# All of the first layer's d_ff blocks by seven products instead of eight, in two interleaved groups, with V and the added exps kept once

## The chip, the cores and the metric

One core of a Trainium2 chip runs the whole program. The metric is the device time of one execution, in microseconds; the kernel before was timed three times.

## What is computed

Attention with RMS-normed q and k, then a two-layer network with a tanh GELU on the attention's output. Eight batches of 12 heads, 448 positions and 64 channels; d_model is 768, d_ff is 2048.

```python
q_n, k_n = (rmsnorm(q, g_q), rmsnorm(k, g_k))
scores = scale * np.matmul(q_n, k_n.transpose(0, 1, 3, 2))
attn = np.exp(scores - np.max(scores, axis=-1, keepdims=True))
attn = attn / (np.sum(attn, axis=-1, keepdims=True) + 1e-09)
x = np.matmul(attn, v)        # heads side by side: 3584 tokens of 768
h = x @ w_in
g = 0.5 * h * (1.0 + np.tanh(c * (h + 0.044715 * h * h * h)))
out = g @ w_out
```

## The kernel before

**Stages.** The program goes batch by batch (0 to 7), in an order written out by hand for every engine (manual_schedule): a batch's attention, then its first layer (x times w_in, GELU). The second layer of the tokens that are already through the first one is spread in small pieces over the next batch's attention, to keep TensorE filled while ACT computes exps. At the very end stands a second-layer block of its own (`final`), for the last 512 tokens.

**Attention.** Heads come in three groups of four (c = 0 to 2). Each group has seven score tiles ("units" 0 to 20 over the batch): four matmuls on 64x64 quarters of the array (L335) write a PSUM tile, ACT turns it into exps (L343). DVE adds six of the seven exp tiles of a group into `es` (steps A, B, F, G: L355, L358, L360, L362), so that the sums over keys take few matmuls (L387 with `ones`); then L387 with `vb` multiplies exps and V, and DVE divides (L397 to L422) and writes x transposed to `xT`. `STEADY` is the order of these steps on TensorE; in it, "5r" stands for five steps of the second layer (L495, four matmuls each), and "u" for a unit. A steady attention begins "5r u 11r uu": five second-layer steps, then unit 0.

**PSUM.** Four tiles of two banks, `rounds`, go round. `pair()` hands out the one that was taken longest ago; a matmul that writes it waits until its last reader is through. The second layer takes the first tile off the list for as long as it accumulates.

**First layer from batch 2 on** (class `Seven`). Eight of 16 blocks of d_ff (0 to 3 and 8 to 11) go by Strassen's scheme in Winograd's form: with w_in and x cut into 2x2 parts, seven products of 12 narrow matmuls (128x224 out, L625) take the place of eight. The sums of w_in parts are formed once (`in_sums`, in `wx`, and `in_place_sum`), the four sums of x parts per batch (`x_sums`, L610 to L613, in `xs`). Products are accumulated in PSUM tiles: X holds product 1, then 1+6, then 1+6+7, then 1+6+7+4; Y holds product 2, Z holds products 5 and 3. ACT copies X at three of these points to SBUF ("keep", L636, into `snaps`), DVE adds copies to Y and Z (L684, L695, L703), and ACT takes four GELUs (L640). The other eight blocks are four `lone` pairs, plain matmuls 448 columns wide (L652, GELU in L658). `early` issues the parts of them that need only the first two thirds of x, while the last third is still being divided; `rest` goes on with the remaining third, and calls side steps by number (`side(0)` to `side(17)`): the work for the next batches that is put between.

**Side work in a first layer of batch b.** Batch b+1's q and k are normed by GpSimd (L278, six operations) and turned by DMA (L319); DVE scales k by the gains (`gain`, L325). Batch b+2's q and k are squared (L162 on ACT, L164 on GpSimd) and totalled on DVE (L173). GpSimd runs its queue in order, and is held back by tiny copies (`gpsimd_waits`, L1035) that read a result it shall not overtake. V is loaded from GpSimd's queue (L147) into `vb`, two tiles in turn, a batch ahead.

**The end.** `token_sums` and `weight_sum` form on DVE the sums for seven products in the last second-layer block (L881 to L884, L873, L875); `final` multiplies (L914) and adds.

Of the kernel before, what the change touches and what calls it, by code (L numbers as in the profile page):

```python
# [17 lines left out]
def kernel(  # L18
# [37 lines left out]
    exq = ctx.enter_context(tc.tile_pool(name="exq", bufs=2))  # L56
    xp = ctx.enter_context(tc.tile_pool(name="xp", bufs=1))
# [51 lines left out]
    vb = [wts.tile([P, HP, NT, D], BF16, name=f"vb{i}") for i in range(2)]  # L109
# [35 lines left out]
    def load_v(b, i, n):  # L145

        nc.gpsimd.dma_start(  # L147
            vb[b % 2][:, i:i + n].rearrange("p a t d -> p a (t d)"),
            v[b, 2 * i:2 * (i + n)].rearrange("(a r) (p t) d -> (r p) a (t d)", r=2, t=NT),
        )  # L150
# [200 lines left out]
    def add_exps(b, c, step):  # L351
        ex = exs[b, c]
        if step == "A":
            es = ess[b, c] = exq.tile([P, 2, 2, S], BF16, tag="es", name="es")
            nc.vector.tensor_add(es, ex[:, :2], ex[:, 2:4])  # L355
# [15 lines left out]
    def products(b, c, what, lo=0, hi=NT):  # L371
# [11 lines left out]
        for i in range(lo, min(hi, n)):  # L383
            for r in range(2):
                rs = slice(r * R, (r + 1) * R)
                for a in range(2):
                    nc.tensor.matmul(  # L387
                        o[r][a * D:(a + 1) * D],
                        vb[b % 2][rs, 2 * c + a, i] if what else ones[rs], es[i][rs, a],
# [180 lines left out]
    wx = wts.tile([128, 3, NCH, FS * 128], BF16, name="wx")  # L570
    fs1, fs2 = slice(0, FS * 128), slice(d_ff // 2, d_ff // 2 + FS * 128)
    LONE = (2, 3, 6, 7)

    def in_sums():

        a11, a21, a12, a22 = wv[:, 0, :, fs1], wv[:, 0, :, fs2], wv[:, 1, :, fs1], wv[:, 1, :, fs2]
        nc.vector.tensor_sub(wx[:, 1], a21, a11)
        nc.vector.tensor_add(wx[:, 0], wx[:, 1], a22)
        nc.vector.tensor_sub(wx[:, 2], a12, wx[:, 0])

    def in_place_sum():

        a21 = wv[:, 0, :, fs2]
        nc.vector.tensor_add(a21, a21, wv[:, 1, :, fs2])

    class Seven:

        def __init__(self, b):
# [6 lines left out]
            self.snaps = [  # L595
                flat[:, n + i * 4 * S:n + (i + 1) * 4 * S].bitcast(F32)
                .rearrange("p (r s) -> p r s", r=2) for i in range(2)
            ]
# [5 lines left out]
            self.lhs = {1: wv[:, 0, :, fs1], 2: wv[:, 1, :, fs1], 4: wv[:, 1, :, fs2],  # L604
                        5: wv[:, 0, :, fs2], 6: wx[:, 0], 7: wx[:, 1], 3: wx[:, 2]}
# [9 lines left out]
        def product(self, i, name, ms=range(NCH)):  # L615
            first = name not in self.tiles
            if first:
                self.tiles[name] = pair("h7")
                self.owner[name] = i
            t, owner = self.tiles[name], self.owner[name]  # L620
            for bank in range(2):
                for n in range(2):
                    at = (bank * 2 + n) * 128
                    for m in ms:
                        nc.tensor.matmul(  # L625
                            t[:, bank, n * QS:(n + 1) * QS],
                            self.lhs[i][:, m, at:at + 128], self.rhs[i][:, m],
                            start=i == owner and n == m == 0,
# [6 lines left out]
        def keep(self, n):  # L635
            nc.scalar.copy(self.snaps[n], self.of("X"))  # L636

        def gelu(self, src, half, tokens):
            lo = self.b % 2 * S + tokens * QS
            nc.scalar.activation(  # L640
                g[:, half * nf // 2:half * nf // 2 + FS, lo:lo + QS],
                src.rearrange("p r (n s) -> p r n s", n=2), AF.Gelu_apprx_tanh,
            )

        def lone(self, i, js, cs, end=False):
            if i not in hs1:
                hs1[i] = pair("hh")
            h = hs1[i]
            for j in js:
                at = (2 * i + j) * 128  # L650
                for c in cs:
                    nc.tensor.matmul(  # L652
                        h[:, j, :S], win[:, c, at:at + 128], xT[self.b][:, c],
                        start=(c == 0), stop=(c == HP - 1),
                    )
            if end:
                lo = self.b % 2 * S
# [664 lines left out]
```

## Time and profile before

| what | us |
|---|---|
| median of three runs (lowest, highest) | 385.64 (385.57, 385.95) |
| the profiled execution | 384.59 |
| its span, from first to last instruction | 382.8 |
| granted TensorE clock, mean | 0.999 |
| a steady first layer (batch 4) | 17.33 |
| a steady attention with second-layer steps (batch 5) | 27.00 |
| first layers of batches 2 to 7 | 17.32 to 17.37 |

The span is split into 40 slices on the page; TensorE is busy for 90% or more in all but the first, second and last. Busy here is the matmul row, whose ends are modelled. The chain of waits is TensorE for 92% of the span, so most other engines' idle time costs nothing by itself. In the lists below a row gives start, length, engine, source line, operation, what is written and read, shapes and count; a bracket at its end gives the idle time before it and who ended that.

### The profile page before, as it was taken

The page shows a single profiled execution, that of the slowest core. Times are in us where ns is not written, and L with a number is a line of the kernel's source. Part 1 is how long each engine was busy: PE and PEld are TensorE (multiplying, and loading weights), DVE is VectorE, ACT ScalarE, POOL GpSimd, SP SyncE. Part 2 cuts the span into 40 slices and gives each one's busy share as a digit, 9 for nine tenths or more (in the row PEclk, how much of TensorE's full clock was granted, in tenths as well). Part 3 has the DMA queues.
Part 4 walks back from the last instruction along what each step waited for, and adds up shares of the span by engine and source line. Part 5 has one row for each costly group of instructions (what it writes and reads, how often), then busy time and mean ns, then how long its engine had stood idle before and what let it go on. Part 6 is the DMA issues. An engine that isn't in the chain of part 4 may idle for free.

```text
span 382.8 us, 14538 instructions
## 1 busy us (share of the span) xinstructions
PE 374.9 (98%) x6508; PEld 273.6 (71%) x6508; DVE 299.4 (78%) x441; ACT 289.6 (76%) x358; POOL 134.1 (35%) x118
## 2 busy tenths in 40 slices
PE   8899999999999999999999999999999999999995
PEld 5565577677878858886678867788678866778563
DVE  4999969995999758895789956996588833899853
ACT  6995589777997689877897789966897659965500
POOL 5997504349203850057401861038400640000000
PEclk9999999999999999999999999999999999999999
DMA  8999999978913996259832897139553340220023
GB/s 255 324 236 210 210 238 235 275 152 190 245 48 77 223 203 112 59 109 260 184 90 53 193 252 117 45 89 222 112 98 84 74 96 15 74 63 3 2 61 105
DMA packets 64594, 54.48 MB, mean 142 GB/s; under 512 B 37652, under 2 KB 60436, under 8 KB 64532
## 3 DMA queue, kind: packets, MB, share of 16 engines
q1 hardware_dynamic: 54016, 41.04, 42.8%
q0 software_dynamic: 10128, 11.80, 18.5%
q8 instruction: 51, 0.84, 0.9%
q10 hardware_dynamic: 388, 0.72, 0.5%
q14 instruction: 11, 0.09, 0.1%
HBM read 45.61 MB, written 11.01 MB: 148 GB/s over the span
## 4 chain that ended last, share of the span: by engine, by line
PE 92%; ACT 5%; DMA 1%; DVE 0%; issue 0%; POOL 0%
PE t L495 33%; PE t L652 14%; PE t L625 13%; PE t L387 9%; PE t L335 8%; PE t L537 5%; PE t L914 5%; ACT ex L343 4%; PE t L556 4%; DMA rawq<-in_q_dram 1%; PE h L436 1%; PE tp L296 1%; PE o L387 0%; DVE ss L173 0%; POOL nrmq L278 0%
## 5 line engine op out<-in xcount | busy, mean ns | idle before, releaser
L343 ACT ACTIVATE ex<-t,shift 128x896 bf16<-128x896 f32 x168 | 156.7, 1013 | 2.9 <-PE t L335 2.2
L495 PE MATMUL t<-wout,g 64*64 64x384 bf16 (+1 forms) x3456 | 150.6, 305 | 0.0
L495 PEld LDWEIGHTS <-g 64*64 64x64 bf16 x3456 | 104.4, 107 | 29.2 <-issue 2.2
L335 PE MATMUL t<-qT,kT 64*64 64x448 bf16 x672 | 57.5, 351 | 1.4 <-ACT ex L343 0.6
L652 PE MATMUL t<-xT,win 128*128 128x448 bf16 x288 | 58.5, 353 | 0.0
L173 DVE TENSOR_REDUCE ss<-sq 128x14 f32<-128x896 f32 (+3 forms) x45 | 43.5, 995 | 18.5 <-ACT sq L162 16.1
L1035 POOL COPY mark<-es 1x1 bf16<-1x1 bf16 x7 | 1.2, 177 | 128.2 <-DVE es L362 119.8
L652 PEld LDWEIGHTS <-win 128*128 128x128 bf16 x288 | 27.7, 98 | 24.1 <-issue 2.1
L278 POOL TENSOR_TENSOR nrmq<-rawq,rinv 128x896 bf16<-128x896 f32 (+1 forms) x21 | 35.4, 1688 | 19.2 <-ACT rinv L205 10.6
L355 DVE TENSOR_TENSOR es<-ex 128x1792 bf16<-128x1792 bf16 x21 | 22.3, 1061 | 16.3 <-ACT ex L343 16.3
L278 POOL TENSOR_TENSOR nrmk<-rawk,rinv 128x896 bf16<-128x896 f32 (+1 forms) x21 | 34.6, 1647 | 0.0
L397 DVE STREAM_TRANSPOSE st<-t 128x448 f32<-128x448 f32 x42 | 24.8, 629 | 10.5 <-PE t L387 9.7
L387 PE MATMUL t<-ex,vb 64*64 64x448 bf16 x588 | 32.3, 350 | 0.0
L335 PEld LDWEIGHTS <-kT 64*64 64x64 bf16 x672 | 23.7, 106 | 9.4 <-issue 1.4
L625 PEld LDWEIGHTS <-win 128*128 128x128 bf16 x288 | 27.6, 98 | 2.7 <-issue 1.0
L658 ACT ACTIVATE g<-t 128x896 bf16<-128x896 f32 x24 | 22.0, 916 | 9.3 <-PE t L652 9.3
L387 PEld LDWEIGHTS <-vb 64*64 64x64 bf16 x672 | 23.3, 107 | 7.9 <-issue 1.2
L409 DVE STREAM_TRANSPOSE rb<-rc 128x896 f32<-128x896 f32 (+1 forms) x25 | 26.7, 1067 | 0.3
L636 ACT COPY xs<-t 128x896 f32<-128x896 f32 x18 | 16.3, 906 | 13.0 <-PE t L625 10.5
L422 DVE TENSOR_TENSOR xT<-t,rb 128x896 bf16<-128x896 f32 x21 | 22.8, 1086 | 0.9
L513 ACT COPY osb<-t 128x768 f32<-128x768 f32 (+1 forms) x18 | 12.6, 703 | 14.0 <-PE t L495 14.0
L164 POOL TENSOR_TENSOR sq<-rawk 128x896 f32<-128x896 f32 (+1 forms) x14 | 22.6, 1614 | 0.7 <-DMA rawk<-in_k_dram 0.7
(147 smaller groups left out, 529.3 us busy)
## 6 DMA issues: line engine op xcount, KB each, us to landing
rawq<-in_q_dram SPq DMA_DIRECT2D x22, 448.0 KB, 4.3
rawk<-in_k_dram SPq DMA_DIRECT2D x22, 448.0 KB, 5.7
out_dram<-osb SPq DMA_DIRECT2D x38, 192.0 KB, 2.9
vb<-in_v_dram POOLq DMA_DIRECT2D x6, 672.0 KB, 7.6
win<-in_moe_w_in_dram POOLq DMA_DIRECT2D x8, 384.0 KB, 11.6
out_dram<-osb SPq DMA_DIRECT2D x31, 96.0 KB, 2.5
wout<-in_moe_w_out_dram POOLq DMA_DIRECT2D x3, 768.0 KB, 18.0
vb<-in_v_dram POOLq DMA_DIRECT2D x2, 448.0 KB, 16.4
```

Of the source, the lines that this page charges most:

```text
L164: eng.tensor_mul(sq, raw, raw)
L173: nc.vector.reduce_sum(sss[b][:, seat(b, c), "qk".index(n), hs, ts], squares(b, c, n, hs, ts), axis=AX.X)
L278: eng.tensor_mul(nrms[n, b, c][:, ts].rearrange("p t a d -> p a t d"), raws[n, b, c][:, :, ts], root[:, :, ts].to_broadcast([P, 2, m, D]),)
L335: nc.tensor.matmul(sc[r * R:(r + 1) * R, a, :S], kT[rs, c, t, r], qT[b][rs, c, :, r], start=True, stop=True,)
L343: nc.scalar.activation(exs[b, c][:, t], scs.pop((b, c, t))[:, :, :S], AF.Exp, scale=scale, bias=shift)
L387: nc.tensor.matmul(o[r][a * D:(a + 1) * D], vb[b % 2][rs, 2 * c + a, i] if what else ones[rs], es[i][rs, a], start=(i == 0), stop=(i == n ...
L397: nc.vector.transpose(st[:, r].rearrange("p a b -> p (a b)"), o[r])
L409: nc.vector.transpose(oas["rb"][:, rs].rearrange("p r s -> p (r s)"), rc.to_broadcast([128, (rs.stop - rs.start) * m, 32]),)
L422: nc.vector.tensor_mul(xT[b][:, 2 * c:2 * c + 2], oas["o", c, 1][:, :, :S], oas["rb"])
L495: mm = nc.tensor.matmul(o[a * R:(a + 1) * R, bank, :hi - lo], g[rs, f, at:at + R], wout[rs, f, lo:hi], start=(n == 0), stop=(n == len(step ...
L625: nc.tensor.matmul(t[:, bank, n * QS:(n + 1) * QS], self.lhs[i][:, m, at:at + 128], self.rhs[i][:, m], start=i == owner and n == m == 0, s ...
L652: nc.tensor.matmul(h[:, j, :S], win[:, c, at:at + 128], xT[self.b][:, c], start=(c == 0), stop=(c == HP - 1),)
```

## The change

- `wx` doubles, and the 16 blocks form two groups, A (blocks 0 to 3 and 8 to 11) and B (4 to 7 and 12 to 15). Both go by seven products; the lone pairs are gone. The products of A and B alternate; a name such as XA is tile X of group A, and "6XA" below is product 6 accumulated into it. Z takes over the tile of Y (`on=`). Each group has three keeps, three adds and four GELUs; group B's copies lie in a further exp tile (`more_snaps`, called `sn`).
- The sums of w_in for B are formed behind those for A, ahead of attentions 1 and 2.
- `vb` and `es` exist once; V is loaded in the attention that uses it, from GpSimd's queue.
- Two of three q and k tiles are squared by GpSimd: c = 0 stays on ACT, q of c = 1 moves from ACT to GpSimd.
- In the next batch's norming, k of c = 0 moves behind the small copy that waits for `xs`; the first DMA transpose and the loads behind it move from side step 2 to 5.
- Of the last block's sums of w_out, two are formed ahead of attention 7; all token sums stand behind the last add of the first layer. Their homes change, as `vb` is one tile now.

```diff
-    vb = [wts.tile([P, HP, NT, D], BF16, name=f"vb{i}") for i in range(2)]
+    vb = wts.tile([P, HP, NT, D], BF16, name="vb")
...
-            es = ess[b, c] = exq.tile([P, 2, 2, S], BF16, tag="es", name="es")
+            es = ess[b, c] = esp.tile([P, 2, 2, S], BF16, tag="es", name="es")
...
+    def in_sums(grp):
+        f1, f2 = blocks_of(0, grp), blocks_of(1, grp)
+        a11, a21, a12, a22 = wv[:, 0, :, f1], wv[:, 0, :, f2], wv[:, 1, :, f1], wv[:, 1, :, f2]
+        s2, s3, s4 = wxs[grp]
+        nc.vector.tensor_sub(s3, a21, a11)
+        nc.vector.tensor_add(s2, s3, a22)
+        nc.vector.tensor_sub(s4, a12, s2)
...
-    def product(self, i, name, ms=range(NCH)):
+    def product(self, i, name, ms=range(NCH), on=None):
         first = name not in self.tiles
         if first:
-            self.tiles[name] = pair("h7")
+            if on:
+                t = self.tiles[on]
+                rounds.append(rounds.pop(next(n for n, x in enumerate(rounds) if x is t)))
+            self.tiles[name] = self.tiles[on] if on else pair("h7")
...
     def early(self):
-        hs1.clear()
         two = range(NCH - 1)
-        self.lone(LONE[0], range(2), early)
-        self.product(1, "X", two)
-        self.product(2, "Y", two)
+        for i, name in ((1, "XA"), (2, "YA"), (1, "XB")):
+            self.product(i, name, two)
...
+            product(1, "XA", one)
+            keep("XA", 0)
+            product(1, "XB", one)
+            keep("XB", 0)
+            product(2, "YA", one)
+            add("YA", 0)
+            product(2, "YB")
+            gelu("YA", 0, 0)
+            product(6, "XA")
+            keep("XA", 1)
+            add("YB", 0)
+            product(6, "XB")
+            keep("XB", 1)
+            gelu("YB", 0, 0)
             side(5)
+            product(5, "ZA", on="YA")
+            product(7, "XA")
+            keep("XA", 0)
+            add("ZA", 0, self.snaps["A"][0])
+            product(7, "XB")
+            keep("XB", 0)
+            self.gelu_kept("A")
             side(8)
+            product(5, "ZB", on="YB")
+            add("ZB", 0, self.snaps["B"][0])
+            self.gelu_kept("B")
+            product(3, "ZA")
+            add("ZA", 1)
+            gelu("ZA", 0, 1)
             side(11)
+            product(4, "XA")
+            gelu("XA", 1, 0)
+            product(3, "ZB")
+            add("ZB", 1)
+            gelu("ZB", 0, 1)
             side(15)
+            product(4, "XB")
+            gelu("XB", 1, 0)
             side(17)
...
-            extra += [("first", lambda: gain(2, 2)), ("first", in_place_sum)]
+            extra += [("first", lambda: gain(2, 2)), ("first", lambda: in_place_sum("A")), ("first", lambda: in_place_sum("B"))]
...
-                   (0, lambda: normed_both(b + 1, 0, nc.gpsimd)),
+                   (0, lambda: normed(b + 1, 0, "q", nc.gpsimd)),
                    (0, lambda: gpsimd_waits(sevens[b].xs[:1, 3, 0, :1])),
+                   (0, lambda: normed(b + 1, 0, "k", nc.gpsimd)),
...
-                m1 += [(15, lambda a=a: squared(b + 2, 1, "q", a)) for a in range(2)]
-                m1.append((15, lambda: square(b + 2, 1, "k", nc.gpsimd)))
-                m1 += [(17, lambda n=n: total(b + 2, 1, n)) for n in "qk"]
+                for c in (1, 2):
+                    m1 += [(11, lambda c=c, n=n: square(b + 2, c, n, nc.gpsimd)) for n in "qk"]
+                m1 += [(11, lambda: total(b + 2, 1, "q")), (17, lambda: total(b + 2, 1, "k"))]
...
-            m1 += [(5, sums_homes), (5, lambda: weight_sum(3)), (5, lambda: weight_sum(2)),
-                   (11, lambda: weight_sum(4)), (17, lambda: token_sums(slice(2, 6))),
-                   (17, lambda: token_sums(slice(0, 2)))]
+            m1 += [(5, lambda: weight_sum(4)), (17, lambda: token_sums(slice(0, 2))),
+                   (17, lambda: token_sums(slice(4, 6))), (17, lambda: token_sums(slice(2, 4)))]
+        if b + 2 == B:
+            extra += [("first", sums_homes),
+                      ("first", lambda: weight_sum(3)), ("first", lambda: weight_sum(2))]
```

What the order becomes is shown at two places. The first is ACT's queue from the last GELUs of batch 2's first layer to the first exps of attention 3; t_100, t_101, t_893 and t_894 are the four PSUM tiles, and each exp reads the tile that its unit wrote. Before:

```order
L640 ACTIVATE g<-t_894 128x4x224
L658 ACTIVATE g<-t_101 128x2x448
L162 ACTIVATE sq<-rawq 128x448 x2
L658 ACTIVATE g<-t_100 128x2x448
L658 ACTIVATE g<-t_893 128x2x448
L1278 ACT_TABLE_LOAD
L343 ACTIVATE ex<-t_101,shift 128x896
L343 ACTIVATE ex<-t_100,shift 128x896
```

Now, where the four tiles are t_103 (YA, then ZA), t_104 (XA), t_895 (XB) and t_896 (YB, then ZB):

```order
L666 ACTIVATE g<-t_103 128x4x224
L666 ACTIVATE g<-t_104 128x4x224
L666 ACTIVATE g<-t_896 128x4x224
L666 ACTIVATE g<-t_895 128x4x224
L1304 ACT_TABLE_LOAD
L344 ACTIVATE ex<-t_895,shift 128x896
L344 ACTIVATE ex<-t_103,shift 128x896
```

Unit 0's tile was that of the GELU third from last; now it is that of the very last one, t_895. The second place is DVE's queue in the same first layer, from the add into the kept copy (`xs`, `sn`) to the first add of exps of the next attention. Before:

```order
L695 TENSOR_TENSOR xs<-t_894,xs 128x896
L703 TENSOR_TENSOR t_894<-t_894,xs 128x2x448
L173 TENSOR_REDUCE ss<-sq 128x14 x2
L325 TENSOR_SCALAR kT<-kT,gcols 128x896
L173 TENSOR_REDUCE ss<-sq 128x14 x2
L325 TENSOR_SCALAR kT<-kT,gcols 128x896
```

Now:

```order
L661 TENSOR_TENSOR xs<-t_103,xs 128x896
L661 TENSOR_TENSOR sn<-t_896,sn 128x896
L661 TENSOR_TENSOR t_103<-t_103,xs 128x2x448
L174 TENSOR_REDUCE ss<-sq 128x14
L661 TENSOR_TENSOR t_896<-t_896,sn 128x2x448
L174 TENSOR_REDUCE ss<-sq 128x14
L326 TENSOR_SCALAR kT<-kT,gcols 128x896
L174 TENSOR_REDUCE ss<-sq 128x14 x2
L326 TENSOR_SCALAR kT<-kT,gcols 128x896
```

A total (L174) of the tile that GpSimd squares now stands between the last two adds (L661 on t_103, that is ZA, and on t_896, ZB); before, both totals stood behind all the adds.

170 lines of the change are left out of this document (73 added, 97 removed).

## The prediction

> **What bounds the kernel now.** I read the page's first part, then busy time by stage (batch 4's first layer, then attention 5; batches count from 0), then that first layer engine by engine.
>
> ```profile
> PE 374.9 (98%) x6508; PEld 273.6 (71%) x6508; DVE 299.4 (78%) x441; ACT 289.6 (76%) x358; POOL 134.1 (35%) x118
> 209.78:227.11 17.33, 17.33 (x137) 12.66 (x140) 12.59 (x15) 12.72 (x17) 12.39 (x9) 1.00 0.88 211
> 227.11:254.11 27.00, 27.00 (x694) 20.46 (x694) 22.64 (x31) 24.20 (x29) 3.96 (x5) 1.00 0.45 98
> ```
>
> TensorE fills both stages (after the length, the columns are PE, PEld, DVE, ACT, POOL, clock), so matmul time taken out counts, unless a wait takes its place. ACT fills 24.20 of 27.00 us of attention: it has little room to start late. The timeline of TensorE in that first layer (start, length, engine, line):
>
> ```profile
> 209.72 1.69 PE L652 MATMUL t<-xT,win 128*128 128x448 bf16 x8
> 211.24 2.46 PE L625 MATMUL t<-xT,win 128*128 128x224 bf16 x24
> 213.54 0.92 PE L652 MATMUL t<-xT,win 128*128 128x448 bf16 x4
> 226.57 0.54 PE L652 MATMUL t<-xT,win 128*128 128x448 bf16 x2
> 227.04 1.01 PE L495 MATMUL t<-wout,g 64*64 64x384 bf16 x20
> 227.88 0.36 PE L335 MATMUL t<-qT,kT 64*64 64x448 bf16 x4
> ```
>
> Eight 448-column matmuls issue in 211.24-209.72 = 1.52 us, 0.190 each. The 24 narrow ones issue from 211.24 until L652 follows at 213.54: 2.30 us, 0.0958 each; their results are there at 213.70, 0.16 after that. The stage runs from 209.72 to 227.04, and unit 0, the first score matmul of the next attention, starts at 227.88, 18.16 us after the stage began. That last number is the yardstick below.
>
> **The saving on TensorE.** The stage's 84 narrow and 48 wide matmuls become 168 narrow ones: 168x0.0958 = 16.09 us against 17.32, so 1.23 us less in each of six batches, 7.4 us in all. Whether it arrives is a question of who must finish before unit 0.
>
> The Trainium skill (TensorE: Matmul & The Clock Gate, Back-to-back issue gap) says that streams of weight load and matmul settle at about 81 ns for 128 columns and 131 ns for 512. Read linearly between these, an estimate by that page, 224 columns take 94 ns and 448 take 123, so 168 narrow ones would cost 15.7 us and the old mix 13.8: a loss of 1.9 us a batch. The rows above have 190 ns for 448, so the trace disagrees and the saving on TensorE stands.
>
> **Unit 0 in batches 2 to 5.** With both groups in flight all four PSUM tiles stay in use to the end, and unit 0 writes the tile of XB, the last to be read: ACT's last gelu must end first. Before, it wrote a tile that ACT had emptied at 224.33. ACT and DVE rows of the stage:
>
> ```profile
> 211.81 1.03 ACT L162 ACTIVATE sq<-rawk 128x448 f32<-128x448 f32 x2
> 213.36 0.91 ACT L636 COPY xs<-t 128x896 f32<-128x896 f32 x1 [0.51 <-PE t L625]
> 222.61 0.92 ACT L640 ACTIVATE g<-t 128x896 bf16<-128x896 f32 x1 [0.77 <-DVE t L703]
> 223.42 0.91 ACT L658 ACTIVATE g<-t 128x896 bf16<-128x896 f32 x1
> 227.15 0.92 ACT L658 ACTIVATE g<-t 128x896 bf16<-128x896 f32 x1 [1.08 <-PE t L652]
> 229.38 1.01 ACT L343 ACTIVATE ex<-t,shift 128x896 bf16<-128x896 f32 x1
> 211.17 1.09 DVE L422 TENSOR_TENSOR xT<-t,rb 128x896 bf16<-128x896 f32 x1
> 212.29 1.05 DVE L610 TENSOR_TENSOR xs<-xT 128x672 bf16<-128x672 bf16 x1
> 213.38 0.51 DVE L611 TENSOR_TENSOR xs<-xT,xs 128x672 bf16<-128x672 bf16 x1
> 214.64 1.09 DVE L684 TENSOR_TENSOR t<-t,xs 128x896 f32<-128x896 f32 x1
> 215.64 1.07 DVE L173 TENSOR_REDUCE ss<-sq 128x14 f32<-128x896 f32 x1
> ```
>
> They give the prices: a gelu lasts 0.92 and lets the next start after 0.81; a keep (L636) 0.91; a PSUM add 1.09, and the next DVE operation may start after 1.00; ACT starts 0.04 after TensorE's end (227.11 to 227.15), which I use behind DVE too. TensorE starts 0.06 after what it waited for (60.42 to 60.48, rows further down). By hand, in the trace's clock:
>
> - TensorE: 24 early matmuls to 212.02; then the third chunk of xT, ready at 212.26, so on at 212.32 (0.30 lost). The first parts of XA, XB and YA end at 213.47, then eleven products of 1.15: YB, 6XA, 6XB, 5ZA, 7XA, 7XB, 5ZB, 3ZA, 4XA, 3ZB, 4XB; 3ZB's results are there at 225.13, 4XB's at 226.28.
> - The rereads between them just fit. ACT's squares end at 212.84, so keep XA runs to 213.8, before 6XA at 214.62; the gelu of YA ends at 216.1, before 5ZA at 216.92; the other keeps have about 1 us. The three keeps and three adds that a batch gains lie beside matmuls here.
> - DVE then has add ZA, the total of q's second tile, and add ZB in its queue. That total waits for a GpSimd square, which used to be ACT's:
>
> ```profile
> 214.99 1.68 POOL L278 TENSOR_TENSOR nrmq<-rawq,rinv 128x896 bf16<-128x896 f32 x1
> 216.64 1.68 POOL L278 TENSOR_TENSOR nrmk<-rawk,rinv 128x896 bf16<-128x896 f32 x1
> 221.73 1.67 POOL L164 TENSOR_TENSOR sq<-rawk 128x896 f32<-128x896 f32 x1
> 213.00 1.22 SPq L319 DMA_TRANSPOSE kT<-nrmk  x1
> rawq<-in_q_dram SPq DMA_DIRECT2D x22, 448.0 KB, 4.3
> vb<-in_v_dram POOLq DMA_DIRECT2D x6, 672.0 KB, 7.6
> 241.47 1.52 PE L387 MATMUL t<-ex,vb 64*64 64x448 bf16 x28
> ```
>
> Behind the wait for xs, four normings take 221.73-214.99 = 6.74, a single one 1.65 to the next. That wait ends some 0.55 earlier (L610 drops from 1.05 to about L611's 0.51, as GpSimd no longer runs a norming beside it), but five normings follow it: 214.44+6.74+1.65 = 222.83, and the square ends at 224.50. The total runs 224.53 to 225.60, so add ZB starts at 225.52 instead of 225.17 and ends at 226.61; gelu ZB starts at 226.65, gelu XB at 227.46, ending at 228.38; unit 0 starts at 228.44. If the normings keep 1.65 throughout, all this is 0.13 earlier. So unit 0 comes 0.43 to 0.56 later than its old 227.88, with all of the saved 1.23 us gone into a wait. I take +0.50 for each of four batches: **+2.0 us**. Bounds: with no total in the way +0.21 (+0.8 in all); with the load of that square late, more: it goes out behind the k transpose, which waits for the first of the five (214.44+1.68+1.22, about 217.4), lands 4.3 us later by the median, 221.7, and is used at 222.83, so it has 1.1 us to spare; I allow a lateness of 1.2 beyond that (+6.8).
>
> Behind unit 0, exp 0 follows the last gelu by 1.31 us as before (228.07 to 229.38), so at 229.69: 1.25 us behind its matmul, where it was 1.50 behind, so attention takes no longer than before. V's load now falls in the batch that uses it: issued behind the last square at about 229.5, landing 7.6 us later, at 237.1, and first used by matmuls at 241.47, before any delay: hidden, 0. The single es tile costs 0: its next writer stands behind DVE transposes that already wait for its readers.
>
> **Batch 6** has no squares or totals: add ZB starts at 225.17, unit 0 at 228.09: **+0.2**. The w_out sums moved ahead of attention 7 (four halves, by L875's 1.75 for a whole one under 1 us each) start about 1 us before unit 0 and end about 2 us before exp 3 does, which DVE waits for: 0, and up to 2 us if DVE got to them later.
>
> **Attentions 1 and 2.** The sums for group B go on DVE ahead of the first add of exps:
>
> ```profile
> 53.17 0.96 DVE L579 TENSOR_TENSOR wx<-win,wx 128x1536 bf16<-128x1536 bf16 x1
> 55.62 1.09 DVE L355 TENSOR_TENSOR es<-ex 128x1792 bf16<-128x1792 bf16 x1 [1.49 <-ACT ex L343]
> 57.01 1.02 DVE L518 COPY osb<-t 128x384 f32<-128x384 f32 x2 [0.24 <-PE t L495]
> 59.79 0.63 DVE L362 TENSOR_TENSOR es<-es,ex 128x896 bf16<-128x896 bf16 x1
> 60.48 0.38 PE L387 MATMUL t<-es,ones 64*64 64x448 bf16 x4
> 99.46 0.94 DVE L584 TENSOR_TENSOR win<-win 128x1536 bf16<-128x1536 bf16 x1
> 100.33 1.08 DVE L355 TENSOR_TENSOR es<-ex 128x1792 bf16<-128x1792 bf16 x1
> PEld L387 <- DVE es L362: 0.6, 2, 0.4
> ```
>
> In attention 1, three more operations of 0.99 end at 57.1 instead of 54.13. DVE had 1.49 of idle time before L355 and 0.24 before L518, so L362 ends 0.97 to 1.2 later, and L387, which starts 0.06 behind it, stalls: **+1.0**. In attention 2 one more operation shifts the chain by 0.87 (99.46 to 100.33), without idle time; the last row says that L387 waited for L362 already there, twice in all: **+0.9**. Both could be smaller (0.5 each) if TensorE waits for something else later in these attentions; I see nothing there.
>
> **The end.** Token sums on DVE start after add ZB (they started beside the last lone blocks):
>
> ```profile
> 360.18 0.92 ACT L658 ACTIVATE g<-t 128x896 bf16<-128x896 f32 x1 [1.35 <-PE t L652]
> 361.61 0.42 DVE L881 TENSOR_TENSOR vb<-g 128x512 bf16<-128x512 bf16 x1
> 363.08 1.75 DVE L875 TENSOR_TENSOR wout<-wout 128x3072 bf16<-128x3072 bf16 x1
> 364.75 0.55 DVE L927 TENSOR_TENSOR osb<-t,osb 128x384 f32<-128x384 f32 x1
> 366.52 0.65 PE L914 MATMUL t<-tw,vb 128*128 128x384 bf16 x3
> ```
>
> Stage 7 starts 132.98 later than the one above. Add ZB frees DVE at 226.17+132.98 = 359.15; four groups of 1.46 (361.61 to 363.08) end at 364.99, the w_out sum (1.73) at 366.72, L927 at 367.27. Product 7 reuses L927's tile: it starts at 367.33, not 366.52: **+0.8**. The first products wait for the last gelu till about 361.07, where they waited till 361.10 before.
>
> **Sum:** 2.0 + 0.2 + 1.0 + 0.9 + 0.8 = 4.9 us on a span of 382.8 (384.59 for the profiled execution; the three timed runs have median 385.64, 1.05 more). So 385.64+4.9 = **390.5 us**, slower by 1.3%.
>
> **Rivals.** (a) Faster: add ZB and gelu ZB are no obstacle (DVE and ACT reach them early), so unit 0 waits for XB's gelu alone: 226.28+0.04+0.92+0.06 = 227.30, 0.58 sooner, five times, and the sums of attentions 1 and 2 and the end are absorbed: 385.64-2.9 = 382.7. For it: DVE is busy only 12.59 of 17.33 us. Against it: the DVE queue above. It decides once the add ends before 225.4. (b) No change: that gain, with +1.0, +0.9 and +0.8 paid: 385.4. (c) Much slower: GpSimd, which gains a square, or its loads run late, and the total holds DVE and so TensorE by 1.2 more in four batches: 395.3. For it: the load that it needs now goes out later, behind the later k tile's transpose. Against: the 1.1 us to spare. (d) The change does what it says to TensorE and nothing waits: 385.64-7.4 = 378.2; the tile that unit 0 needs speaks against it.
>
> **Chances.** Forecast 0.70, (a) 0.09, (b) 0.07, (c) 0.12, (d) 0.02. The bounds of the terms (0.8 to 6.8, 0 to 0.4, 1.0 to 2.1, 0.3 to 1.2) span 2.1 to 10.5; the forecast's own middle is 388.5 to 392.5, and the range that leaves out 2 in 10 is 386.6 to 393.5. About 0.2%, 0.77 us, is what a measurement of this kernel can tell from none: faster 0.11, same 0.07, slower 0.82.
>
> **What would show it.** Right: in the first layers of batches 2 to 5 TensorE issues 0.096 us matmuls, then idles about 1.1 us before L336 (the score matmuls), released by ACT's last gelu; ACT's last two gelus stand back to back behind a DVE add that follows a total released by POOL; TensorE idles about 1 us before the first es matmul of attentions 1 and 2, and 0.7 before the second of the w_out sums' products. Wrong: unit 0 within 17.7 us of the stage's start, or idle time at the keeps and adds between the products.

## The result, and the profile after

| | us |
|---|---|
| before, median of four runs | 385.66 (385.57 to 385.95) |
| changed, median of four runs | 409.50 (406.83 to 419.96) |
| changed against before | 1.059 times, 95% interval 1.055 to 1.064 |
| the profiled execution of the change, and its span | 406.83, 404.9 |

The ratios here and below leave out runs that are over 1.5% longer than the fastest of their kernel, such as the 419.96, though a wait of the kind found here can make such a run by itself (the 391.31 of number 7). The change is 22.1 us longer by the spans (404.9 against 382.8), where the prediction had 4.9. Two rows of the changed kernel's page: the busy times, and the scaling of k by its gains (`gain`, now L326) on DVE.

```profile
PE 376.0 (93%) x6724; PEld 306.4 (76%) x6724; DVE 331.4 (82%) x470; ACT 302.4 (75%) x368; POOL 140.2 (35%) x122
L326 DVE TENSOR_SCALAR kT<-kT,gcols 128x896 bf16<-128x896 bf16 x19 | 28.2, 1491 | 9.2 <-DMA kT<-nrmk 9.2
```

The gain is the same operation on the same data as before, and its mean has gone from 819 ns to 1491. Where the time lies shows in the busy times by stage of the changed kernel: length, then PE, PEld, DVE, ACT, POOL, clock. A stage begins with a first layer's first matmul and the next one with unit 0 of the attention behind it; these are the first layers of batches 2 to 6, with attention 3 after the first of them.

```profile
122.54:141.28 18.74, 17.41 (x192) 16.62 (x189) 16.02 (x19) 15.46 (x20) 14.73 (x10) 1.00 0.73 172
141.28:167.43 26.15, 26.15 (x672) 21.97 (x672) 21.91 (x30) 23.25 (x28) 3.26 (x5) 1.00 0.52 118
167.43:193.89 26.46, 19.85 (x192) 17.91 (x189) 22.41 (x20) 15.56 (x20) 15.70 (x11) 0.87 0.65 165
220.04:238.79 18.75, 17.41 (x193) 16.62 (x190) 16.02 (x19) 15.47 (x20) 14.57 (x10) 1.00 0.74 169
264.94:289.11 24.17, 19.19 (x192) 17.65 (x189) 20.76 (x20) 15.57 (x20) 15.75 (x11) 0.93 0.68 142
315.26:337.80 22.54, 19.20 (x192) 17.64 (x189) 16.12 (x18) 13.49 (x16) 10.84 (x8) 0.92 0.61 101
```

All five took 18.16 us before. Batches 2 and 4 take 0.58 and 0.59 longer, which is the prediction's step for them. Batches 3, 5 and 6 take 8.30, 6.01 and 4.38 longer, 18.69 together, with the clock below full: that is the miss. What TensorE waited for (us in total, times, longest):

```profile
PE t L648 <- DVE xs L661: 12.0, 3, 5.6
PE t L336 <- ACT g L666: 5.0, 5, 1.2
PE t L938 <- DVE osb L951: 0.6, 1, 0.6
```

L648 are the products and "xs L661" is add ZA, the add into the kept copy, which must be done before product 3ZA may write its tile. Three waits, one in each of the three long stages. Batch 3 on DVE and GpSimd (start, length, engine, line; in brackets the idle time before and who ended it):

```profile
173.82 2.07 DVE L174 TENSOR_REDUCE ss<-sq 128x14 f32<-128x896 f32 x2
176.80 7.17 DVE L326 TENSOR_SCALAR kT<-kT,gcols 128x896 bf16<-128x896 bf16 x1 [0.91 <-DMA kT<-nrmk]
183.89 1.08 DVE L661 TENSOR_TENSOR xs<-t,xs 128x896 f32<-128x896 f32 x1
...
172.18 1.68 POOL L279 TENSOR_TENSOR nrmk<-rawk,rinv 128x896 bf16<-128x896 f32 x1
173.82 1.68 POOL L279 TENSOR_TENSOR nrmq<-rawq,rinv 128x896 bf16<-128x896 f32 x1
175.47 1.68 POOL L279 TENSOR_TENSOR nrmk<-rawk,rinv 128x896 bf16<-128x896 f32 x1
177.12 1.68 POOL L279 TENSOR_TENSOR nrmq<-rawq,rinv 128x896 bf16<-128x896 f32 x1
178.76 1.68 POOL L279 TENSOR_TENSOR nrmk<-rawk,rinv 128x896 bf16<-128x896 f32 x1
180.41 1.67 POOL L165 TENSOR_TENSOR sq<-rawq 128x896 f32<-128x896 f32 x1
182.04 1.67 POOL L165 TENSOR_TENSOR sq<-rawk 128x896 f32<-128x896 f32 x1
```

The gain starts when the transposed k is there and lasts 7.17 us, where one alone lasts 0.44. GpSimd runs seven operations without a pause; the last ends at 183.71, and the gain ends 0.26 behind it, at 183.97. Behind the gain in DVE's queue stands add ZA, and TensorE stands still. That costs more than the wait; stretches of the same batch:

```profile
180.00:182.00 2.00, 0.00 (x0) 0.00 (x0) 2.00 (x1) 0.00 (x0) 2.00 (x2) 1.00 1.25 228
182.00:184.00 2.00, 0.00 (x0) 0.00 (x0) 2.00 (x2) 0.00 (x0) 1.71 (x2) 0.75 0.96 285
184.00:185.00 1.00, 0.00 (x0) 0.00 (x0) 1.00 (x2) 0.00 (x1) 0.00 (x0) 0.50 1.19 344
188.00:189.00 1.00, 1.00 (x7) 0.80 (x6) 1.00 (x2) 0.41 (x1) 0.00 (x0) 0.50 1.05 403
189.00:190.00 1.00, 1.00 (x8) 0.81 (x7) 0.54 (x1) 0.81 (x2) 0.38 (x1) 0.59 0.53 192
190.00:191.00 1.00, 1.00 (x13) 1.00 (x12) 0.02 (x1) 0.61 (x1) 1.00 (x1) 1.00 0.00 0
```

TensorE has been idle since 179.39. The granted clock is 1.00 up to 182.00 and 0.50 from 184.00 on; its mean of 0.75 between them puts the fall near 183.0, 3.6 us into the idle time. TensorE goes on at 185.02, and the clock stays at 0.50 until near 189.8 (0.59 is the mean of the us from 189.00): three products take 2.19, 2.24 and 1.33 us instead of 1.15 each. So 5.63 us of waiting and 2.3 of slow matmuls make the loss.

The rest is where the prediction had it. Batch 4: DVE, then ACT, then TensorE.

```profile
234.88 1.09 DVE L174 TENSOR_REDUCE ss<-sq 128x14 f32<-128x896 f32 x1 [0.56 <-POOL sq L165]
235.89 1.09 DVE L661 TENSOR_TENSOR t<-t,sn 128x896 f32<-128x896 f32 x1
237.01 1.73 ACT L666 ACTIVATE g<-t 128x896 bf16<-128x896 f32 x2 [0.92 <-DVE t L661]
238.79 0.38 PE L336 MATMUL t<-qT,kT 64*64 64x448 bf16 x4 [1.21 <-ACT g L666]
```

A total released by GpSimd, add ZB behind it, two gelus back to back, unit 0 behind the last. In attention 1 the es matmuls wait for DVE. In attention 2 a score matmul does, for a copy (osb) out of the PSUM tile that it writes (second row). The next two rows are the lengths of attentions 1 and 2 of the changed kernel, the last two those of the kernel before:

```profile
61.27 0.38 PE L388 MATMUL t<-es,ones 64*64 64x448 bf16 x4 [0.65 <-DVE es L363]
103.87 0.38 PE L336 MATMUL t<-qT,kT 64*64 64x448 bf16 x4 [0.68 <-DVE osb L514]
...
50.15:76.20 26.05, 25.31 (x579) 19.20 (x581) 24.93 (x43) 22.90 (x28) 5.79 (x7) 1.00 0.85 228
95.49:122.54 27.05, 26.37 (x679) 20.82 (x669) 24.18 (x32) 23.63 (x29) 2.77 (x4) 1.00 0.60 129
```
```profile
50.33:75.41 25.08, 25.08 (x578) 18.71 (x579) 22.30 (x40) 22.60 (x28) 6.32 (x8) 1.00 1.04 256
94.72:121.00 26.28, 26.28 (x681) 20.81 (x669) 23.17 (x31) 23.57 (x29) 2.76 (x4) 1.00 0.59 131
```

### The profile page after: what moved, and what is told of

Same layout as the page of the kernel before. It is cut to its first block, busy times and chain, and to the rows that moved or that the text cites. A ratio compares the mean times of both kernels' runs of the same rounds, so it can differ in the third digit from the quotient of the medians.

```text
span 404.9 us, 15043 instructions
## 1 busy us (share of the span) xinstructions
PE 376.0 (93%) x6724; PEld 306.4 (76%) x6724; DVE 331.4 (82%) x470; ACT 302.4 (75%) x368; POOL 140.2 (35%) x122
## 4 chain that ended last, share of the span: by engine, by line
PE 49%; DVE 28%; ACT 8%; issue 6%; DMA 5%; POOL 2%; SPq 1%; DVEq 0%; POOLq 0%
PE t L496 18%; PE t L648 14%; PE t L336 5%; ACT ex L344 5%; PE t L557 4%; DVE st L398 4%; DVE xT L423 4%; PE t L388 3%; PE t L938 3%; DMA rawk<-in_k_dram 2%; DVE ss L174 2%; DVE rb L410 2%; ACT g L666 2%; DVE es L359 2%; DVE es L356 2%
## 5 line engine op out<-in xcount | busy, mean ns | idle before, releaser
L496 PEld LDWEIGHTS <-g 64*64 64x64 bf16 x3456 | 111.4, 107 | 20.5 <-issue 1.1
L648 PEld LDWEIGHTS <-win 128*128 128x128 bf16 x576 | 56.5, 101 | 5.1 <-issue 3.9
L648 PEld LDWEIGHTS <-wx 128*128 128x128 bf16 x432 | 43.0, 101 | 13.6 <-issue 12.5
L174 DVE TENSOR_REDUCE ss<-sq 128x14 f32<-128x896 f32 (+3 forms) x45 | 43.8, 995 | 8.5 <-ACT sq L163 5.0
L666 ACT ACTIVATE g<-t 128x896 bf16<-128x896 f32 x36 | 32.0, 917 | 15.4 <-DVE t L661 15.1
L336 PEld LDWEIGHTS <-kT 64*64 64x64 bf16 x672 | 25.2, 106 | 15.1 <-issue 8.6
L326 DVE TENSOR_SCALAR kT<-kT,gcols 128x896 bf16<-128x896 bf16 x19 | 28.2, 1491 | 9.2 <-DMA kT<-nrmk 9.2
L648 PE MATMUL t<-xs,win 128*128 128x224 bf16 x288 | 34.5, 274 | 0.0
L648 PE MATMUL t<-xT,win 128*128 128x224 bf16 x288 | 29.6, 259 | 0.8
L648 PE MATMUL t<-xT,wx 128*128 128x224 bf16 x144 | 18.6, 287 | 12.0 <-DVE xs L661 12.0
L648 PE MATMUL t<-xs,wx 128*128 128x224 bf16 x288 | 29.6, 259 | 0.0
```

Source lines behind the costliest of these rows:

```text
L174: nc.vector.reduce_sum(sss[b][:, seat(b, c), "qk".index(n), hs, ts], squares(b, c, n, hs, ts), axis=AX.X)
L326: nc.vector.tensor_scalar(kT[:, c], kT[:, c], gcol[:, 0:1], None, op0=ALU.mult)
L336: nc.tensor.matmul(sc[r * R:(r + 1) * R, a, :S], kT[rs, c, t, r], qT[b][rs, c, :, r], start=True, stop=True,)
L496: mm = nc.tensor.matmul(o[a * R:(a + 1) * R, bank, :hi - lo], g[rs, f, at:at + R], wout[rs, f, lo:hi], start=(n == 0), stop=(n == len(step ...
L648: nc.tensor.matmul(t[:, bank, n * QS:(n + 1) * QS], lhs[:, m, at:at + 128], self.rhs[i][:, m], start=i == owner and n == m == 0, stop=n == ...
L666: nc.scalar.activation(g[:, f:f + FS, lo:lo + QS], (self.of(name) if src is None else src).rearrange("p r (n s) -> p r n s", n=2), AF.Gelu ...
```

## The experiments

Run again several times beside these, the kernel before had a median of 384.7 to 385.5 us. "Held" means a gain of k's first tile that lasts over 2 us; a boundary is the end of one GpSimd operation with the next right behind it.

**1. The gain behind the last add.** `(5, lambda: gain(b + 1, 0))` becomes `(15, ...)`.

> The gain of k's first tile moves from ahead of add ZA (side step 5) to behind the last add ZB (side step 15). Theory T1 (the gain waits for a gap in GpSimd's unbroken run and holds the adds behind it): TensorE no longer idles ahead of product 3ZA; every first layer of batches 2 to 5 takes about 18.75 us from its start to unit 0 (batches 2 and 4 took 18.74 and 18.75 in the changed kernel, 3 and 5 took 26.46 and 24.17), batch 6 about 18.4 instead of 22.54; 17.5 us less than the profiled 406.83, so 389.3. Rival T2 (the transposed k or its load lands late in batches 3, 5, 6): the gain is late at its new place too, but unit 0 needs it only 7 us later, so also about 389; told from T1 by the strided gain. Rival T3 (the square, total and gelu chain at the end of the layer is what costs): nothing changes, 405 to 411.

Measured: 391.01 us (1.0145 times before, 1.011 to 1.018), clock 1.00, first layers of batches 2 to 5 of 18.58 to 18.59 us, batch 6 of 18.39. T3 falls; T1 and T2 both gave 389, and the next two kernels tell them apart. No gain is held here. That the time is 0.5 us from the prediction's 390.5 is in part luck: attention 7 takes 27.72 us here and 26.15 in the change. In this kernel the last gain ahead of it waits for its k; the w_out sums and a copy out of PSUM stand behind that gain on DVE, and the scores wait 1.35 us for the copy.

**2. The gain in strides.**

```diff
-        nc.vector.tensor_scalar(kT[:, c], kT[:, c], gcol[:, 0:1], None, op0=ALU.mult)
+        t = kT[:, c].rearrange("p t r s -> p (t r s)").rearrange("p (n two) -> p two n", two=2)
+        nc.vector.tensor_scalar(t, t, gcol[:, 0:1], None, op0=ALU.mult)
```

> The gain keeps its place and its numbers, but reads and writes every second element (two passes over 448), so that the VectorE operation isn't in its fast form (0.44 us). T1 (only the fast form has to get in between GpSimd's instructions): every gain takes about 1 us whatever GpSimd does, none 3.84 to 7.17; first layers of batches 2 to 5 about 18.75 us to unit 0, 389 to 390.5 in all. T2 (late data): the gain of batches 3, 5, 6 still ends 3 to 7 us late, 405 to 411.

Measured: 425.28 us (413.74 to 425.67). Alone such a gain takes 0.70 to 0.75 us and not the expected 1, and all five were held. Batch 3, DVE and the last GpSimd operation of the run:

```profile
185.69 7.45 DVE L327 TENSOR_SCALAR kT<-kT,gcols 128x896 bf16<-128x896 bf16 x1 [0.91 <-DMA kT<-nrmk]
...
190.95 1.67 POOL L165 TENSOR_TENSOR sq<-rawk 128x896 f32<-128x896 f32 x1
```

It ends 0.52 behind GpSimd's run (193.14 against 192.62), as each of the first three did: not late data, but the guess that strides would keep it clear of GpSimd was wrong.

**3. GpSimd pauses for the gain.**

```diff
-                   (0, lambda: normed_both(b + 1, 2, nc.gpsimd)),
...
+            m1 += [(5, lambda: gain(b + 1, 0)), (5, lambda: gpsimd_waits(kT[:1, 0, 0, 0, :1])),
+                   (5, lambda: normed_both(b + 1, 2, nc.gpsimd)),
```

> GpSimd pauses after four of its normings behind the xs mark... in its queue, a copy that reads the scaled kT stands ahead of the normings of the third tile (c = 2), so that GpSimd stops until the gain is done. T1: the gain ends about 0.26 us after the norming beside which it started, in every batch, never 3 us or more; GpSimd loses about 0.5 us, which the square's total passes on to unit 0: stages of 18.8 to 19.3, 389 to 391.5. T2: GpSimd then waits for late data too, and the stages of batches 3, 5, 6 get no shorter: 405 or more.

Measured: 393.07 us (1.018 times, 1.015 to 1.022). The time is above its range of 389 to 391.5. The five gains last 0.56 to 0.60, the stages 19.12 to 19.14, batch 6's 18.39; attention 7 takes 27.33, for the reason of number 1. T2 falls: with GpSimd standing, the data are there.

**4. k normed first again.** `normed(b + 1, 0, "k", nc.gpsimd)` back ahead of the copy that waits for `xs`.

> k of the first tile is normed ahead of the xs mark again, as before the change; all the rest is the change. The transposed k is then there when VectorE's totals end, and the gain starts directly behind them, as before the change, where it got in at the first boundary between two GpSimd operations five times of five. T1 with arrival (it is lost when VectorE stood idle waiting for the transpose): no long gains, 387 to 390. T1 with length alone (the run of GpSimd, now longer, decides): gains of 3 to 7 us stay in some batches, 400 to 411.

Measured: 388.47 us (1.007 times, 1.004 to 1.010), gains of 1.59 and, in batch 6, 1.93. One norming's place set off nearly all the holds (number 7, with k normed first too, still has one). The stages are 18.39 now, since the squares come earlier as well and no total holds up add ZB.

**5. The gain 0.9 us later.** A `reduce_sum` over 128x512 of the transposed k, result unused, ahead of the gain.

> The changed kernel with one VectorE operation more: a sum over a part of the transposed k (128x512, some 0.6 us, its result unused) stands ahead of the gain, so that the gain comes up some 0.6 us later, about 0.25 us behind a boundary between two GpSimd operations instead of 0.3 ahead of one. Theory T1a (it is lost when it comes up about 0.3 us ahead of a boundary, and a transpose that always takes about 2.9 us from the end of the norming puts it there each time): every gain ends 0.26 us behind the next boundary, 1.6 us long, none over 2; TensorE waits 0 to 0.6 us a batch for the later add ZA; 389 to 393. Rival T1b (lost whenever VectorE stood idle ahead of it, or whenever GpSimd's run is this long): gains of 3 to 7 us in most batches, 405 or more.

Measured: 422.25 us (1.098 times, 1.095 to 1.101); the gains came up 1.2 to 1.3 us ahead of a boundary and all five were held (3.12 to 6.46). T1a falls.

**6. Only the late norming, in the kernel before.**

```diff
-                   (0, lambda: normed_both(b + 1, 0, nc.gpsimd)),
+                   (0, lambda: normed(b + 1, 0, "q", nc.gpsimd)),
                    (0, lambda: gpsimd_waits(sevens[b].xs[:1, 3, 0, :1])),
+                   (0, lambda: normed(b + 1, 0, "k", nc.gpsimd)),
```

> The kernel before with nothing of the change but this: k of the first tile is normed behind the xs mark. T1a: its transpose lands about 2.9 us after the norming, so the gain comes up about 0.3 us ahead of a boundary in five batches and is lost in most of them, until GpSimd's run of five operations (3.3 for batch 6) ends: gains of 4 to 7 us, 4 to 6 us of TensorE waiting at the add into the kept copy for each, 395 to 414. Rival (the lock-out needs the longer run with two squares, or the products of the change): gains under 2 us, 385 to 388.

Measured: 401.29 us (393.66 to 405.85; 1.029 times, 1.022 to 1.036). In the profiled execution, the 393.66, one gain of five is held, for 2.43 us in batch 3, whose stage takes 23.39 us; the others take 18.77. In that batch k came some 1.5 us later than in the others (DVE idle for 3.17 us ahead of the gain, elsewhere in batches 2 to 5 for some 1.7), and the gain met GpSimd's fourth boundary instead of the third. Neither the products nor the added squares are needed for a hold.

**7. Three mends on top of number 4.** XB's tile goes to the end of `rounds`, so that unit 0 takes ZA's; `in_sums("B")` moves into batch 1's first layer and `in_place_sum("B")` behind the first es adds; `weight_sum(1)` goes between the first adds of `final`.

> The kernel with k normed first (388.47 us) and three edits more: unit 0 takes the tile of ZA and XB's tile goes to the third unit; the w_in sums of group B are formed in batch 1's first layer and their in-place sum behind the first group of exps of attention 2; the last w_out sum goes between the first two adds of the last block. By the prediction's terms: 1.0 and 0.8 of attentions 1 and 2 and 0.6 of the end come back, and 0.2 to 0.4 in each of five batches, where unit 0 no longer waits for the last gelu and the exps become the bound: 384 to 385.5, about as before the change or 0.4% faster. If the exps do not bound, up to 1 us a batch more: 381.

Measured: 385.38 us (385.28 to 398.54; 1.0013 times, 0.9998 to 1.0029), about as before. In the profiled execution, 391.31, one gain is held (6.52), although k is normed first. Unit 0 comes 17.36 us after the stage's start, but the stages and attentions together only go from 44.33 to 44.08: the exps are the bound there, as the first of them starts 19.66 us after the stage's start in both kernels, behind ACT's gelus. The w_in sums in batch 1 cost 2.0 us (28.26 from attention 2's unit 0 to batch 2's first matmul, against 26.28).

**8. The change once more.**

> The changed kernel once more, unchanged. T1: the gain of k's first tile comes up at the same place against GpSimd's operations in every batch, and is lost in some batches for as long as the run lasts, not always the same ones: 400 to 425 us, with the time following from the number of lost batches at 4 to 8 us each.

Measured: 410.51 us. Held are batches 2, 4 and 5 (7.12, 7.17, 5.52), not 3 and 6, at the same place in the queues.

**9 and 10. Two other delays.** As number 5, with sums over 128x128 and 128x896.

> As the kernel with the added sum, with 128 columns instead of 512 (some 0.2 us): the gain comes up about 0.1 us ahead of a GpSimd boundary. Theory P (the moment against the boundary decides): all five batches alike, lost or got in. Theory R (chance at each first boundary): some of each. Theory D (a gain that waited on a semaphore rather than queued behind a running VectorE operation is mostly lost): four or five lost, 415 to 425 us.

> As before, with 896 columns (some 1.05 us): the gain comes up about 0.85 us ahead of a boundary, where the gains of the kernel before (0.69 to 0.85 us ahead, directly behind a total) got in ten times of ten. Theory P: it gets in in all five batches, gains of 1.1 us, 390 to 393. Theory R: some of each. Theory D: four or five lost, 415 to 425 us.

Measured: 422.94 and 422.11 us, ten of ten held (2.74 to 6.86). P falls with the second, whose gains came up 0.84 to 0.89 ahead of a boundary, and R with both.

**11. VectorE kept busy until k is there.** `for n in "qk"` becomes `"qkkk"` in the totals ahead of the gain.

> The changed kernel with the second of the two totals ahead of the gain done three times (the same sums once more), so that VectorE is still busy when the transposed k lands, and the gain starts directly behind a running operation, about 0.9 us ahead of a GpSimd boundary, nothing else changed. Theory D (a gain that is queued directly behind a running VectorE operation mostly gets in at the next boundary, one that waited on a semaphore mostly does not): the gains of batches 2 to 5 take about 1.2 us, three or four of four; batch 6, which has no totals, stays as in the changed kernel (0.6 or 3.8 us); 389 to 394 us. Rival (chance alone, or anything else that the change moved in GpSimd's queue): two or more of the four are lost, 5 to 7 us each, 400 or more.

Measured: 419.65 us, all four held although each stood directly behind a running VectorE operation; D falls. They also came up later, at the fourth boundary instead of the third. Batch 3, DVE and the GpSimd operation beside which the gain comes up:

```profile
183.39 3.31 DVE L174 TENSOR_REDUCE ss<-sq 128x14 f32<-128x896 f32 x3
186.62 5.93 DVE L326 TENSOR_SCALAR kT<-kT,gcols 128x896 bf16<-128x896 bf16 x1
...
185.69 1.68 POOL L279 TENSOR_TENSOR nrmq<-rawq,rinv 128x896 bf16<-128x896 f32 x1
```

**The count.** Four theories had gone wrong, so I counted, over the twelve profiles with the gain at its place and in its own form (before, after, 4 to 11 and the two that follow), every boundary at which a gain of k's first tile was waiting, by its place in GpSimd's unbroken run:

| boundary of the run | got in | did not |
|---|---|---|
| first or second | 12 | 0 |
| third | 15 | 9 |
| fourth | 1 | 32 |
| fifth and sixth | 3 | 40 |

The gains of number 9 (the sum over 128x128) that came up within 0.02 us of the third boundary are counted from the fourth on. The three late ones that got in are all at the sixth boundary of batch 5.

The kernel before meets the second (first in batch 6), the change the third, and most of the delayed ones the fourth. This gave theory Q and two more kernels; their eight gains of batches 2 to 5 and two of batch 6 are in the table.

**12. A later boundary.** Number 4 with `"qkkk"` in the totals.

> The kernel with k normed first (gains of 1.59 us, all got in), and the second total ahead of the gain done three times, so that the gain comes up some 2 us later in GpSimd's run. Theory Q (GpSimd leaves VectorE an opening at the first three boundaries of an unbroken run, and none from the fourth on): the gain now meets the fourth boundary, between the normings and the squares, and is lost in batches 2 to 5, 3 to 5 us each, until the run ends; 393 to 405 us. Rival (the norming of k behind the xs mark is what loses it, or chance): it gets in as in that kernel, 0.3 to 1.7 us, 388 to 391.

Measured: 410.38 us. Three of the four are held, 4.27 us each, and one got in at the fourth boundary (1.00): "none" was too strict. The time is over the range, as each held stage took 24.7 to 25.3 us instead of 18.39.

**13. GpSimd's run begun anew.** Number 11, with one copy on GpSimd behind k's norming that waits for the first total.

```diff
-                   (0, lambda: normed_both(b + 1, 1, nc.gpsimd)),
-                   (0, lambda: normed_both(b + 1, 2, nc.gpsimd)),
...
+                m1 += [(5, lambda: total(b + 2, 0, "q")),
+                       (5, lambda: gpsimd_waits(sss[b + 2][:1, 0, 0, 0, :1]))]
+                m1 += [(5, lambda c=c: normed_both(b + 1, c, nc.gpsimd)) for c in (1, 2)]
+                m1 += [(5, lambda: total(b + 2, 0, "k"))] * 3
...
```

> The kernel with the total done three times (gains of 4.3 to 5.9 us, none of batches 2 to 5 got in), and one GpSimd copy more: behind k's norming it waits for the first of the totals, so that GpSimd stands for about 1 us and its unbroken run starts again with the second tile. The gain comes up at the same moment. Theory Q: it now meets the second or third boundary of a run and gets in in batches 2 to 5, under 1.7 us each; batch 6, whose queue is not changed, gets in or is lost by 3.8 us; 389 to 395 us. Rival (what stands ahead of the gain on VectorE, or chance): lost as before, 410 to 420.

Measured: 404.55 us. Batch 3, GpSimd and then DVE:

```profile
178.25 0.18 POOL L1059 CAST mark<-ss 1x1 bf16<-1x1 f32 x1 [1.17 <-DVE ss L174]
178.40 1.68 POOL L279 TENSOR_TENSOR nrmq<-rawq,rinv 128x896 bf16<-128x896 f32 x1
180.04 1.68 POOL L279 TENSOR_TENSOR nrmk<-rawk,rinv 128x896 bf16<-128x896 f32 x1
181.69 1.83 POOL L279 TENSOR_TENSOR nrmq<-rawq,rinv 128x896 bf16<-128x896 f32 x1
...
181.27 0.70 DVE L326 TENSOR_SCALAR kT<-kT,gcols 128x896 bf16<-128x896 bf16 x1
```

The gain stands behind the same totals as in number 11, one norming earlier in the queue, and gets in at the run's second boundary in four of four batches; the GpSimd operation that it got ahead of lasts 1.83 instead of 1.68. Counted without the pause this is the third place, where 15 of 24 got in, so four of four could also come by chance, about once in seven times. Batch 6, whose queue is as in the change, is held for 3.85. The time missed its range: the pause makes the squares late, unit 0 comes at 20.09 us, where TensorE has idled for 2.02 us, and its clock is 0.57 to 0.59 in the four us behind that in batches 2, 3 and 4 (1.00 in batch 5, after the same idle time).

**14. Mended, with a pause in the right place.** This kernel was made ahead of numbers 11 to 13. Number 7 with GpSimd's copy that reads the scaled k ahead of its last norming, so behind the third operation of the run; one of B's w_in sums in batch 0's first layer, the two others ahead of attention 1.

> The mended kernel, with three further edits: a GpSimd copy that reads the scaled kT stands ahead of the last norming (k, c = 2), so that GpSimd stops until the gain is done; of group B's three w_in sums the first goes into batch 0's first layer, where VectorE waited 1.15 us for a transpose, and the two others stand ahead of attention 1 again. Theory T1: no gain over 1.7 us in any run, so no run 4 us or more above the others; attention 1 loses at most 0.2 us, batch 1 with attention 2 comes back from 28.26 to 26.3-26.6 us; steady periods stay at 44.1 us against 44.33 before the change: 383.3 to 384.5, some 0.3% below the kernel before. If GpSimd's pause delays the squares, up to 0.4 us a batch more: 385.5.

Measured: 383.74 us (383.40 to 384.04), before 385.53; 0.9953 times, 0.9934 to 0.9971. The gains take 1.59 (batch 6: 1.93), the time from attention 2's unit 0 to batch 2 is 26.42. GpSimd and DVE in batch 4:

```profile
217.68 1.68 POOL L279 TENSOR_TENSOR nrmq<-rawq,rinv 128x896 bf16<-128x896 f32 x1
219.74 0.18 POOL L1063 COPY mark<-kT 1x1 bf16<-1x1 bf16 x1 [0.38 <-POOL nrmq L279]
...
218.02 1.59 DVE L326 TENSOR_SCALAR kT<-kT,gcols 128x896 bf16<-128x896 bf16 x1
```

The pause costs GpSimd 0.38 us. No gain is held in the profile, and the six runs lie within 0.64 us of each other. All seven products in both groups are in this kernel; of the 7.4 us that they save on TensorE, 1.8 are left as the gain over the kernel before.

## Why the prediction was wrong

- **The saving on TensorE, 7.4 us: right in size.** Where nothing waits (number 4), 4XB's results are there 16.59 us after the layer's start; the hand schedule had 226.28-209.72 = 16.56.
- **Unit 0, +0.50 in batches 2 to 5: right** where no gain is held, 0.58 and 0.59, by the mechanism named. The lower bound of 0.21, with no total in the way, showed in number 4: 0.23. Batch 6, predicted at +0.2, has the same 0.23 there and in number 1.
- **Attentions 1 and 2, +1.0 and +0.9: right in size,** 0.97 and 0.77. In attention 1 the wait is the one named, for es; in attention 2 it is not: the es matmuls wait for nothing, and a score matmul waits 0.68 us for DVE's copy out of PSUM. That DVE delays both by about as much is luck. **The end, +0.8: right,** 0.85 (40.95 us from the last first layer's start, 40.1 before). V's load and the single es tile cost nothing, as said: attentions 3 to 6 take 26.15 us against 26.16.
- **"The rereads between them just fit … The three keeps and three adds that a batch gains lie beside matmuls here": this step failed.** It took the adds to start when their operands are there. In batches 3, 5 and 6 add ZA stood behind the gain, and the gain behind GpSimd: 7.71, 5.42 and 4.15 us more than these stages take without a hold (18.75 in batch 4; 18.39 for batch 6 in number 1), 17.3 in all. The other 4.8 of the 22.1 are what the sum had as 4.9. The gain had no term in the sum at all. It was moved, too: its k is normed one operation later, so it meets GpSimd's run one boundary later.
- **The row that should have stopped me** is in the profile of before (DVE, then GpSimd, batch 4):

```profile
217.63 0.94 DVE L325 TENSOR_SCALAR kT<-kT,gcols 128x896 bf16<-128x896 bf16 x1
218.96 1.09 DVE L695 TENSOR_TENSOR xs<-t,xs 128x896 f32<-128x896 f32 x1 [0.39 <-ACT xs L636]
...
218.29 1.83 POOL L278 TENSOR_TENSOR nrmq<-rawq,rinv 128x896 bf16<-128x896 f32 x1
```

An operation of 0.44 us lasts 0.94, ends 0.25 behind a GpSimd norming (218.32), and the norming behind it is longer by 0.15: the two engines take turns. Once seen, the question is what happens when DVE doesn't get its turn. One operation's wait, 1.7 us, could have been priced from this row; that it can last for the whole run no row of before shows.

The Trainium skill (SBUF — State Buffer, Who interferes with whom) says that a VectorE operation in a mode that uses two ports and a GpSimd operation shut each other out, and that the second waits until the first has finished. The trace agrees at the first two boundaries of a run, 12 of 12. By that sentence, as an estimate from the rows here, the gain would have lasted at most 1.68+0.44 = 2.1 us; the trace has 7.17, over five GpSimd operations, and the measurement decides.

- **Of the rivals,** (c) had the right chain, GpSimd to DVE to TensorE, but with the total as the link, at 1.2 us a batch. It was bounded by how late the data could be, and the hold isn't lateness of data (number 3). The sign that the prediction named for its being wrong, idle time at the keeps and adds between the products, is what came.

What stays open: why GpSimd leaves an opening at the first two boundaries and almost none from the fourth on. That its queue is by then filled ahead would fit, but no run shows it. At the third boundary it is a matter of chance as far as these traces resolve (changed kernel: two of five got in, twice, in other batches). Of the gains that came up some 1.3 us ahead of it, directly behind a running VectorE operation, 7 of 8 got in; of those that had waited for k and came up 0.3 us ahead, 8 of 16. That is too few to tell whether either matters there.

## What to carry to other kernels

A VectorE operation on bf16 in SBUF that lasts longer beside GpSimd than alone is a warning: count how many GpSimd operations run without a wait around it, and put it where it meets the first or second boundary, or make GpSimd wait for it. Price the operations in a queue that an edit did not touch as well, if what they wait for has moved. And where an engine's spare time hides an edit, look at the worst instance of each operation ahead of it in that queue, not at its mean.

## What the runs showed of the hardware

- A waiting VectorE scaling was let in at 12 of 12 first and second boundaries of an unbroken GpSimd run, 15 of 24 third ones and 4 of 76 later ones, and otherwise ran when the run ended. No phase of a GpSimd operation was safe to come up in (0.3, 0.75, 0.87 and 1.25 us ahead of the third or fourth boundary were all held), nor was a place directly behind a running VectorE operation (1 of 8 got in at the fourth boundary).
- In batch 3 the granted clock fell to 0.50 some 3.6 us into TensorE's idle time, and came back some 4.8 us after it went on. The Trainium skill (TensorE: Matmul & The Clock Gate, Part 1) has half rate after an idle window of about 3.4 us, and full rate after as much work. The trace agrees there only roughly, and elsewhere it does not: the clock also fell behind 2.02 us of idle time, in three batches of four (number 13), and the measurement decides. The wait of 5.63 us cost 7.9.
- A gain over every second element (0.72 us alone, against 0.44) was held five times of five, where the plain one was held three times of five: a somewhat slower form alone does not take an operation out of GpSimd's way.
